# Two PSUM banks in one instruction: merged exponentials, normalisations and clamped sums in an attention and feed-forward kernel

## The chip, the cores and the metric

The kernel runs on one core of a Trainium2 chip. The metric is device time in microseconds, the median of several executions. The engines are TensorE (PE, with its weight loads shown as PEld), VectorE (DVE), ScalarE (ACT), GpSimd (POOL) and SyncE (SP); PSUM, into which TensorE writes, has eight banks of 512 float32 for each of 128 partitions.

## The reference

```python
# q, k, v: (4, 8, 768, 64); n_global 8, n_local 96
scores = scale * np.matmul(q, k.transpose(0, 1, 3, 2))
is_global = pos[None, :] < int(n_global)
is_local = (rel >= 0) & (rel < int(n_local))
keep = is_global | is_local
dist = np.where(is_global & ~is_local, float(n_local), np.abs(rel))
slopes = 2.0 ** (-8.0 * (np.arange(H) + 1) / H)
scores = scores - slopes[:, None, None] * dist[None, :, :]
scores = np.where(keep, scores, -1000000000.0)
scores = scores - np.max(scores, axis=-1, keepdims=True)
a = np.exp(scores)
a = a / (np.sum(a, axis=-1, keepdims=True) + 1e-09)
attn = np.matmul(a, v)                        # (4, 8, 768, 64)
x = attn.transpose(0, 2, 1, 3).reshape(3072, 512)
h = np.maximum(x @ w_in, 0.0)                 # w_in (512, 2048)
out = h * h @ w_out                           # w_out (2048, 512)
```

## The kernel before

The 3072 rows are worked in eight halves of 384 rows (three tiles of 128), two for each batch element. For each half the kernel loads q, k and v, turns q and k (the first batch on TensorE, later ones by transposing DMAs), forms the scores of each tile with its own block of keys and the block before (whose first 32 columns are replaced by the global keys), takes exponentials, multiplies them by a mask that holds the bias, multiplies by v, divides by the sum, and turns the result into `xt`. Layer 1 multiplies `xt` by w_in, clamps at zero and squares into `h2`; layer 2 multiplies by w_out. From the third half on, layer 1 is done by a scheme with seven block products in place of eight (`layer1_group`), and most of layer 2 too (`layer2_pair`); sums of inputs and of weights are formed on VectorE for them.

**Order.** The kernel lists its work twice. First, functions such as `score_unit`, `attend` or `layer1_group` list operations in a `Plan`: `plan.pe` for products on TensorE (numbered p0, p1, ...), `plan.add` and `plan.after` for work of the other engines (a number in one common list; its letter tells the engine: a ScalarE, d VectorE, s SyncE, g GpSimd) and `plan.load` for loads in GpSimd's queue (l0, l1, ...). `ORDER` is a table, and `by_table` emits the operations in its order; `l40^227` is a load that also waits for operation 227. Each engine works through its own entries in that order. The loads of the opening are numbered by `LOADING`, so that l1 to l3 are k and q of tiles 3 and 2, l7 and l8 q and k of tile 5, and l11, l13, l16 and l17 the four quarters of w_in.

**PSUM.** A product that begins an accumulation takes one or two banks. `idle_banks` (L225) sorts the banks whose readers are all done by the time at which they became idle, and takes the first ones. Each bank is a tile of its own, under the tag `ps0` to `ps7` (`bank`). Semaphores are placed by the framework, from which tiles an instruction reads and writes.

**The work around the change.**
- `score_unit` (L697) and, for the first batch, `score_tile` (L1390) write scores into two banks, one for each of two heads. Two `ACTIVATE` instructions (L721; L1426) take the exponentials, one for each bank.
- `attend` (L754) multiplies by v into one bank for each pair of heads. `norm` takes the reciprocal of the sums (L778) and multiplies (L781), once for each of the four pairs of heads. `to_x_by_dma` turns two of them at a time with one DMA (L796).
- `layer1_group` has the products p1, p5, p2, p6, p3, p7, p4. Bank "a" receives p1, then p6, p7 and p4; bank "c" a copy of p1's sum and p2; bank "f" p5 and p3. `keep` copies a partial sum to SBUF. p3 and p7 each end with a clamped sum on VectorE, `add_relu` (L990): the bank plus the kept partial sum, clamped at zero. p4 writes into bank "a" again, and needs p7's clamped sum to be done. Squares (L1012, L1014) follow when both parts of a block are there.

Of the kernel before, what the change touches and what calls it, by code (L numbers as in the profile page):

```python
# [9 lines left out]
FP32 = mybir.dt.float32  # L10
# [4 lines left out]
P = 128  # L15
# [33 lines left out]
ORDER = """d1 g2 a4 s8 p0 s10 a6 d12 a0 d13 l2 l1 a18 l3 d3 a30 d17 d15 d20 l4 a25 d14 a29 d9 a16 l0 d19 a26  # L49
d22 d21 d5 a23 p2 a28 l10 d11 p1 a24 p5 d7 l5 p3 l6 p10 d31 a32 a33 d34 l9 p6 a27 d35 p9 a39 p8 l8  # L50
d44 p11 d36 a40 p7 d43 l7 p4 a46 p13 d37 a41 p14 d45 l11 p12 d48 a42 p16 p17 d59 a47 l12 p15 a52 p25
d51 p19 l13 a49 d38 p28 p24 d55 a53 p20 l14 d69 p23 d64 a50 p34 d65 a60 l16 p31 d56 p21 a81 p22 d72
p27 l15 a61 p29 d58 p30 a57 p26 d70 a82 p33 l17 d68 p18 a71 a77 p35 d66 l23 p36 p32 d54 a86 d67 a85
p40 d62 p39 l18 d63 a97 d91 a73 p41 l19 d84 a78 d83 a74 p37 d79 l20 a98 d75 p44 l22 p38 d107 l21 d80
p47 d76 a89 p52 p48 d96 l27 a92 d111 p42 a93 l28 d106 a112 p43 l29 a119 p46 a113 d105 p45 a101 l30
d110 p53 d103 p55 p50 a120 p59 a90 d95 d116 a87 d100 p51 d99 d94 p57 d122 p54 d125 p65 p63 p49 d135
d121 p67 d146 a114 d128 a102 p61 p62 a104 d132 d117 a88 p75 d108 a129 p83 d115 a142 d109 p60 d209
a143 d118 d189 p64 a130 d273 d193 a138 p70 a136 p72 d159 p82 a133 d194 p71 d187 a134 p56 d160 a131
d190 a162 p69 d137 a186 p81 d161 l33 a123 d212 p74 d139 a165 d163 l25 a188 d156 p84 d205 a166 l31
d151 p73 a169 a184 d157 p85 l35 d206 a164 d167 a171 d147 p58 a168 l36 d196 p80 d124 l34 a126 p89  # L60
d148 p88 a181 p86 l32 d210 a202 d150 a182 p76 l24 d158 a170 d183 p77 a172 l26 d152 p87 a203 d174
a199 l37 p78 d154 a197 p79 p66 d204 a200 l38 a127 d207 p68 d185 a178 d149 a179 p90 a140 d180 p91
a213 d208 a175 d144 p94 a173 d201 a176 p92 d153 s220 d237 p100 a215 d195 a155 p102 s221 d211 d238
a214 p96 a224 d177 p95 a241 a141 p98 d225 p104 a216 s198 d226 p93 p97 a246 d223 a217 s227 a218 p103
d230 d222 p99 s231 a245 d240 p110 d239 p108 s219 l43 p111 a256 d244 a249 l44 p106 a257 d259 a250
d236 l40^227 p109 d247 p116 d228 p101 a252 l45 d251 a269 d258 p115 l41 a270 p114 d242 p113 a253 d192
l42 a262 d255 p117 a265 d232 p105 l46 d191 a272 a260 d233 p123 a266 l48^220 p118 a263 d280 p121 p122
d235 a274 l39 d234 p132 a278 d268 p128 a145 d279 p130 a287 d264 p126 a292 p127 d271 p125 a290 s327
p134 a285 d267 p139 d286 p135 d283 p133 a302 p136 s248 l47 d254 a295 p129 d296 s328 p143 a288 d293
p141 a284 p138 d297 p142 d304 p140 a289 p124 d300 s229 p137 a303 d294 p120 a306 d281 p146 a305 p144  # L70
d277 p147 a311 p131 a301 d307 p107 s282 d298 a329 p145 d291 p148 a309 p112 a308 d312 a399 d314 p151
p152 d313 p156 l51^282 s299 a330 p149 d310 p119 d315 a331 d322 a341 p150 s243 d316 a333 s261 l49^231
d275 a342 p168 d317 p165 a321 l52 a334 p153 d318 p155 a355 l53 a336 d332 p154 a337 d323 l50 d319
a359 p170 d324 l54 p160 d320 a361 p172 a350 p174 d338 a364 p161 p163 d366 a351 p164 a326 p176 d325
d340 p166 d436 p158 d369 a354 d335 a339 p169 a347 d356 p178 a367 p157 d360 p159 a371 d343 a344 p171
d348 a345 p181 d353 p180 s402 l56^327 a362 p182 a375 d374 p173 a372 p184 d346 p186 s403 a365 p162
d376 a357 p188 a382 d352 p192 d363 a380 p167 p179 a385 d391 s276 p175 s377 a373 p189 d358 a368 p190
a404 p185 d386 p193 s392 d388 d381 p183 p191 d393 a387 p187 l63 d389 p196 a383 p177 d390 a413 l59
p194 d378 a370 d384 a414 l74 p201 d379 a409 p202 p195 a423 l58 p199 d405 a426 d415 l62 p198 a427
d406 a424 d395 l55^377 p206 a410 d407 p200 a437 d416 l61^403 a421 d396 p211 a411 d408 p197 a420 l60  # L80
d397 p203 d481 p212 a417 d429 p204 a422 l75 d425 a445 a418 d484 p207 l66 d412 p205 a444 a438 d433
l57 a430 p213 d428 p216 d435 a446 d400 p220 l65 s434 a431 p214 p219 a455 d447 p215 a454 p227 d450
a448 s496 p222 d398 p225 d485 p218 a449 d486 p217 a461 d432 p210 a464 s497 a452 d419 a458 p224 d482
p231 a401 d460 p228 p229 d465 s349 l64 p221 a442 a453 p226 d466 p235 d456 p232 a462 p223 d469 a475
p239 d483 a451 d467 a571 p234 d459 a457 p208 p233 d473 a489 p237 a494 p209 d470 s474 a471 p230 d439
p241 a468 d440 a498 p242 s394 d478 s443 a500 s441 d463 p236 p238 d476 p249 a479 d472 p245 p244 a517
p240 d488 a501 d487 a505 p247 d499 a506 d477 l73^441 s495 a508 p246 d513 a518 d492 l71 d480 a509
p258 p248 d490 a533 l70 d511 p243 d519 p251 a514 l69 d491 a515 d520 p252 a502 p265 l72 p262 d542
a503 p260 p253 a538 l67 d536 p270 a525 p266 d507 a527 p267 l68 a543 d510 p257 a528 p268 d548 a532
p255 p271 d544 a530 p261 d493 a549 p273 d545 a546 p259 d537 p269 a552 p274 d534 p275 d516 p264 p276  # L90
a540 d547 p278 a556 p272 d554 a553 p254 a550 d535 s575 p250 a551 d559 d504 p282 s576 d521 p283 a565
p279 d523 a529 p281 a524 p277 d522 a563 p284 p286 d566 d560 p287 d568 a578 a567 d557 p280 p291 a564
d541 s558 d555 p263 d577 p285 p256 s526 d561 s512 p293 d583 a531 d569 p295 d595 a602 d539 p296 p292
a604 d570 a605 p298 d598 a596 a607 s597 p288 d599 s562 a608 p290 d606 p294 a585 d601 a586 p301 s574
d579 a592 d600 s573 a603 p297 a617 d609 p289 d614 p303 a588 d610 s584 d587 a593 s572 p306 a611 d580
d619 p307 a612 d623 p299 a589 d663 p310 p308 a615 d582 a624 d613 p300 d664 a625 p304 a629 p315 d590
a616 p312 d591 a621 p323 d581 d631 a635 p309 p302 a645 d627 p311 a618 p329 d630 p316 a628 p319 d594
p317 a636 p313 d640 p327 d637 a632 p305 a653 p321 d638 a650 p333 d622 a642 p322 p330 a644 d659 p320
p318 d654 p314 s660 a639 p325 d633 p326 a648 p332 d634 p335 s626 d658 s655 p324 d649 p331 d646 p334
p336 d656 a661 d641 a643 p328 p346 a667 d668 p351 a651 d682 p338 d657 a698 a692 d670 p353 d669 p355  # L100
d671 p357 d703 p337 a706 d665 a652 p361 d701 p350 a674 d711 p347 a672 p359 a673 d666 p363 p339 d708
d693 a697 p358 a647 p340 d707 a713 a662 p354 d677 p364 d675 p349 d683 a715 p342 s676 d702 d684 p352
p356 d699 a696 p362 p367 d687 a712 p365 d678 s688 p360 d704 a716 s620 p343 d714 a709 d710 p371 d679
p369 d685 p341 d705 d724 a719 p366 a689 d680 p368 a686 d717 p372 a700 p345 d720 d725 p370 d718 a691
p373 a721 p344 d737 d727 a726 d681 p348 d722 p374 d723 p383 d738 a728 p385 d756 a729 p377 a690 d733
p375 a741 d740 a759 d734 p378 d739 d694 d735 s695 p380 d730 d752 d736 p376 d742 d748 p379 d749 a731
d751 s732 d753 p381 p388 d754 p387 p386 a743 d744 a762 d755 a761 d745 p382 s746 p390 d747 p391 d760
p384 d765 d750 d764 p394 s766 a757 p389 a771 a772 s758 p392 d763 p393 d767 d769 s768 s770"""
# [28 lines left out]
class Plan:  # L137
# [7 lines left out]
    ENTER = 0.19  # L145
# [117 lines left out]
    def run(self):  # L263
        order = []
        self.in_rows = False
        for e, op in self.by_table() if ORDER else self.by_rank():
# [9 lines left out]
            if op.move is not None:  # L276
                there, long, back = op.move
                self.last_move = start
                self.landed = max(end + there, self.landed) + long
                op.done = self.landed + back  # L280
# [18 lines left out]
def kernel(  # L299
# [44 lines left out]
    def bank(shape, dtype, name, i=0):  # L344
        return ps_p.tile(shape, dtype, name=name, tag=f"ps{plan.now[i]}")
# [71 lines left out]
    def warm_up(e):  # L417
        ps = bank([P, 512], FP32, "warm")
        for _ in range(8):
            nc.tensor.matmul(ps, lhsT=zero[:, 0:P], rhs=zero, start=True, stop=True)  # L420
# [217 lines left out]
    def turn(x, a):  # L638
        state = {}

        def emit(e):
            state["ps"] = trp = bank([P, 2, HT, P], FP16, "trp")
# [54 lines left out]
    def score_unit(x, unit):  # L697
        bt, sp = x.bt, []
# [217 lines left out]
    def layer1_group(x, g):  # L916
# [69 lines left out]
        def give(job, name, which, n, kept=None):  # L986
# [20 lines left out]
            if len(done) < 2:  # L1007
                return ready
# [676 lines left out]
```

## Time and profile before

| | |
|---|---|
| median of 3 runs | 200.1 us (200.0 to 201.06) |
| profiled execution | 200.26 us, span 198.5 us |
| TensorE | 190.9 us busy (96%), 2428 matmuls, granted clock 0.999 |
| VectorE | 178.7 us (90%), 445 instructions |
| ScalarE | 153.6 us (77%), 332 instructions |
| GpSimd | 66.6 us (34%), 82 instructions |
| DMA | 27.53 MB, mean 139 GB/s |

The profile is of one execution. The span runs from the first to the last instruction; 1.76 us of that execution's time lie outside of it. A line of the groups names the kernel's line, the engine, the operation, what it writes and reads, how often, its busy time, the mean duration in ns, and the idle time of the engine ahead of it with what ended it. Busy time of TensorE counts overlapping matmuls once.

### The profile page before, as it was taken

To read this page: it belongs to the slowest core of one execution; us is meant where nothing else is said; L and a number is where in the kernel's file an instruction comes from. 1 tells how busy PE (TensorE), PEld (TensorE's weight loads), DVE (VectorE), ACT (ScalarE), POOL (GpSimd) and SP (SyncE) were. 2 spreads that over 40 slices of the span, in tenths; PEclk is the share of its full clock that TensorE was granted. 3 is DMA by queue.
4 is the path that set the end of the run, shared out by engine and by line. 5 is a ranking of instruction groups with operands and counts; after the bars stand their busy time and mean duration, and the time that the engine had idled before them with its cause. 6 is when DMAs were issued, how large, how long until landed. Compare 5 with 4: busy or idle time off the path is not lost.

```text
span 198.5 us, 6069 instructions
## 1 busy us (share of the span) xinstructions
PE 190.9 (96%) x2428; PEld 166.7 (84%) x2428; DVE 178.7 (90%) x445; ACT 153.6 (77%) x332; POOL 66.6 (34%) x82
## 2 busy tenths in 40 slices
PE   7997999999999999999999999999999999999992
PEld 2775988866987897799989997999889998999992
DVE  7898898999998999998999997999999998898842
ACT  6798766989897989999999987976599758366210
POOL 8996544098006900920696000910000000000000
PEclk9999999999999999999999999999999999999999
DMA  5999999999999999998999996999542050120223
GB/s 160 178 148 191 196 183 170 207 196 155 137 211 125 126 135 271 175 142 138 180 149 150 134 195 166 84 105 156 153 129 81 3 132 5 53 106 3 106 82 132
DMA packets 106604, 27.53 MB, mean 139 GB/s; under 512 B 96720, under 2 KB 103632, under 8 KB 106576
## 3 DMA queue, kind: packets, MB, share of 16 engines
q0 software_dynamic: 74944, 13.11, 86.0%
q1 hardware_dynamic: 30432, 13.45, 33.9%
q10 hardware_dynamic: 1200, 0.59, 1.1%
q8 instruction: 19, 0.31, 0.7%
q14 instruction: 9, 0.07, 0.1%
HBM read 27.26 MB, written 6.29 MB: 169 GB/s over the span
## 4 chain that ended last, share of the span: by engine, by line
PE 83%; DMA 5%; POOL 4%; DVE 4%; ACT 1%; issue 1%; POOLq 0%; DVEq 0%
PE yps L1143 32%; PE hps L929 28%; PE hps L818 9%; PE sp L708 4%; PE av L769 4%; DMA w_mix<-in_k_dram 4%; PE yps L1059 4%; POOL w_mix L488 2%; DMA xt<-tm 2%; POOL v L488 1%; DVE tm L1471 1%; DVE vb L354 1%; PE trp L646 1%; DVE hr L990 1%; POOL sk L488 1%
## 5 line engine op out<-in xcount | busy, mean ns | idle before, releaser
L1143 PEld LDWEIGHTS <-h 128*128 128x128 f16 x376 | 33.9, 98 | 4.1
L721 ACT ACTIVATE ex<-sp 128x512 f16<-128x512 f32 x66 | 35.6, 615 | 1.5 <-PE sp L708 1.3
L929 PEld LDWEIGHTS <-w_in_sb 128*128 128x128 f16 x384 | 32.4, 98 | 2.1 <-issue 0.5
L1143 PEld LDWEIGHTS <-mixed 128*128 128x128 f16 x272 | 25.3, 98 | 3.0
L488 POOL DMA_DIRECT2D v<-in_v_dram x24 | 21.5, 921 | 16.5 <-DMA xt<-tm 16.2
L990 DVE CUSTOM_DVE_ANT_0 hr<-hps,kept 128x384 f16<-128x384 f32 x48 | 25.2, 553 | 1.4 <-ACT y L352 0.5
L929 PEld LDWEIGHTS <-in_mix 128*128 128x128 f16 x288 | 24.3, 98 | 0.6 <-DVE x_mix L908 0.3
L488 POOL DMA_DIRECT2D sq<-in_q_dram x19 | 17.0, 900 | 21.9 <-DMA q<-sq 20.3
L488 POOL DMA_DIRECT2D sk<-in_k_dram x19 | 17.1, 907 | 20.9 <-DMA xt<-tm 11.7
L818 PE MATMUL hps<-xt,w_in_sb 128*128 128x256 f16 (+2 forms) x224 | 23.4, 258 | 0.0
L929 PE MATMUL hps<-xt,w_in_sb 128*128 128x192 f16 x192 | 22.8, 246 | 0.2 <-DMA xt<-tm 0.2
L996 ACT ACTIVATE hr<-hps 128x384 f16<-128x384 f32 x35 | 17.0, 496 | 7.6 <-PE hps L929 7.1
L352 ACT COPY y<-yps 128x256 f32<-128x256 f32 (+2 forms) x36 | 12.9, 369 | 12.7 <-PE yps L1143 12.5
L352 ACT COPY kept<-hps 128x384 f32<-128x384 f32 x41 | 19.0, 491 | 4.6 <-PE hps L929 3.9
L1143 PE MATMUL yps<-w_mix,h 128*128 128x256 f16 (+1 forms) x192 | 22.6, 264 | 0.0
L929 PE MATMUL hps<-x_mix,w_in_sb 128*128 128x192 f16 x192 | 22.1, 246 | 0.3 <-DVE hr L990 0.3
L1143 PE MATMUL yps<-w_out_sb,h 128*128 128x256 f16 (+1 forms) x184 | 22.4, 268 | 0.0
L1143 PE MATMUL yps<-w_mix,mixed 128*128 128x256 f16 (+1 forms) x184 | 22.2, 268 | 0.0
L929 PE MATMUL hps<-x_mix,in_mix 128*128 128x192 f16 x192 | 21.9, 246 | 0.0
L745 DVE TENSOR_TENSOR phat<-ex,mask 128x1024 f16<-128x1024 f16 (+1 forms) x36 | 20.9, 597 | 0.3 <-ACT ex L721 0.3
L818 PEld LDWEIGHTS <-w_in_sb 128*128 128x128 f16 x224 | 17.7, 98 | 3.6 <-DMA w_in_sb<-in_moe_w_in_dram 0.2
L1012 ACT ACTIVATE h<-hr 128x768 f16<-128x768 f16 x23 | 19.3, 846 | 0.1
(112 smaller groups left out, 378.5 us busy)
## 6 DMA issues: line engine op xcount, KB each, us to landing
out_dram<-y SPq DMA_DIRECT2D x23, 256.0 KB, 2.5
v<-in_v_dram POOLq DMA_DIRECT2D x24, 128.0 KB, 6.4
sk<-in_k_dram POOLq DMA_DIRECT2D x19, 128.0 KB, 5.4
sq<-in_q_dram POOLq DMA_DIRECT2D x19, 128.0 KB, 5.9
w_in_sb<-in_moe_w_in_dram POOLq DMA_DIRECT2D x4, 512.0 KB, 11.2
w_out_sb<-in_moe_w_out_dram POOLq DMA_DIRECT2D x4, 512.0 KB, 10.7
y<-in_k_dram ACTq DMA_DIRECT2D x2, 256.0 KB, 4.9
y<-in_q_dram SPq DMA_DIRECT2D x2, 256.0 KB, 4.3
```

What stands on the lines that cost most here:

```text
L352: nc.scalar.copy(out=out, in_=in_)
L488: dma = nc.gpsimd.dma_start(out=dst, in_=src[x.b, :, r0 + t * P:r0 + (t + 1) * P, :] .rearrange("h p d -> p h d"))
L708: nc.tensor.matmul(sp[h][:, i, :], lhsT=lhsT, rhs=x.q[rows, r % HT, a, :], start=i == 0, stop=True, skip_group_check=True)
L721: nc.scalar.activation(out=st["ex"][:, h], in_=sp[h], func=AF.Exp, scale=scale)
L745: eng(e).tensor_tensor(out=x.phat[a][:, :, t0:t0 + n], op=ALU.mult, in0=st["ex"][:, :, i0:i0 + 2 * n].rearrange("p e (t b) c -> p e t (b c ...
L769: nc.tensor.matmul(av[:, h, j, :], lhsT=lhsT, rhs=rhs, start=h == 0 and (j, before) == blocks[0], stop=before or r == 0, skip_group_check= ...
L818: nc.tensor.matmul(st["ps"][:, i * n:(i + 1) * n], lhsT=w_in_sb[:, kk, m * P:(m + 1) * P], rhs=x.xt[:, kk, c0:c1], start=i == kk == 0, sto ...
L929: nc.tensor.matmul(st[name][:, i * HC:(i + 1) * HC], lhsT=left(i, kk), rhs=right(kk), start=fresh > 0 and i == kk == 0, stop=kk == KK - 1, ...
L990: nc.vector._custom_dve(TENSOR_ADD_SAT, out=hidden(which)[:, :, cols], in0=sums(name), in1=st[kept], s0=LARGEST, s1=0.0)
L996: nc.scalar.activation(out=o, in_=i, func=AF.Relu)
L1012: nc.scalar.activation(out=h2, in_=hr, func=AF.Square)
L1143: nc.tensor.matmul(st[bank_name][:, 0:n], lhsT=a(m), rhs=b(m)[:, cols], start=fresh > 0 and m == 0, stop=m == HK - 1, skip_group_check=not ...
```

## The change

All of PSUM becomes one tile of eight banks, and `bank` gives out a view of one of them. `two_banks` gives a view of two banks, whichever they are. With it, one instruction reads both banks: one exponential for the two heads of a score unit, one reciprocal and one product for two pairs of heads, and one clamped sum for p3 and p7 together (`give_two`, which waits for both products and both kept sums). The normalisation is listed at the second `attend` of its pair; its DMA waits for that one operation. The kept sums and the hidden values (`hr`) of a group lie in one tile each, and the exponentials of the first batch are masked in place. `ORDER` is replaced as a whole (1164 entries where there were 1244); the planner adds 0.6 us (`LATER`) to its expected landing times once they pass 15 us, and its costs for the merged operations are 0.87 to 1.13 us. `LOADING`, `OPENING`, `PLACES` and `idle_banks` stay.

```diff
-    def bank(shape, dtype, name, i=0):
-        return ps_p.tile(shape, dtype, name=name, tag=f"ps{plan.now[i]}")
+    banks = ps_p.tile([P, 8, 512], FP32, name="ps", tag="ps")
+
+    def bank(shape, dtype, i=0):
+        flat = banks[:, plan.now[i]]
...
+    def two_banks(i, j, n):
+        return banks[:, i::j - i][:, 0:2, 0:n]
...
-        for h in range(2):
-            def exp(e, h=h):
...
-                nc.scalar.activation(out=st["ex"][:, h], in_=sp[h], func=AF.Exp, scale=scale)
-            exps.append(plan.add({"ACT": 0.505}, exp, [job] + exps))
+        def exp(e):
+            st["ex"] = phat_p.tile([P, 2, 4, P], FP16, name="ex", tag="ex", bufs=4)
...
+                                 in_=two_banks(*held, 4 * P), func=AF.Exp, scale=scale)
+        exps = [plan.after(job, {"ACT": 0.87}, exp)]
...
-        x.norms[a] = plan.after(job, {"DVE": 0.74}, norm)
+        x.norms[pair] = plan.after(jobs[0], {"DVE": 1.13}, norm, jobs[1:])
+        jobs[1].users[0].append(x.norms[pair])
...
+        def give_two(one, two):
+            def add_relu(e):
+                ps = two_banks(st["held", "f"], st["held", "a"], 2 * HC)
+                nc.vector._custom_dve(
+                    TENSOR_ADD_SAT, out=hidden()[:, :, :, HC:2 * HC],
+                    in0=ps.rearrange("p b (m c) -> p b m c", c=HC),
+                    in1=st["kept"].rearrange("p b (m c) -> p b m c", c=HC), s0=LARGEST, s1=0.0)
+            op = plan.after(two, {"DVE": 0.96}, add_relu, [one, ops["kept", 0], ops["kept", 1]])
...
         def p3():
-            job = run("f", 0, mixed_weight(3), plain(1, 1), [ops["keep5"], in_mix_ops[g][3]])
-            give(job, "f", 0, 1, "keep2")
+            ops["p3"] = run("f", 0, mixed_weight(3), plain(1, 1),
+                            [ops["kept", 1], in_mix_ops[g][3]])

         def p7():
-            job = run_mixed("a", 0, mixed_weight(2), 2, [ops["keep2"], in_mix_ops[g][2]])
-            ops["c22"] = give(job, "a", 1, 1, "keep5")
+            job = run_mixed("a", 0, mixed_weight(2), 2, [ops["kept", 0], in_mix_ops[g][2]])
+            ops["c22"] = give_two(ops["p3"], job)
```

The first loads, in the order of the old and of the new table (k2 is tile 2 of k, c1 the second quarter of w_in; tiles 0 and 1 of q and k come by other queues):

```
before: k2 k3 q2 v0 v1 k4 q3 q4 v2 k5 q5 c1 v3 c0 v4 c3 v5 c2
after:  q2 k2 v0 q3 k3 v1 k4 q4 v2 c2 q5 k5 v3 c1 v4 c0 v5 ... c3
```

More of the change, by code (lines that the diff above doesn't have):

```diff
@@ L278, in run @@
                 self.last_move = start
[L279 removed]
+                before, self.landed = self.landed, max(end + there, self.landed) + long
+                self.landed += self.LATER if before <= 15.0 < self.landed else 0.0
                 op.done = self.landed + back
@@ L417, in warm_up @@
     def warm_up(e):
-        ps = bank([P, 512], FP32, "warm")
+        ps = bank([P, 512], FP32)
         for _ in range(8):
@@ L697, in score_unit @@
     def score_unit(x, unit):
-        bt, sp = x.bt, []
+        bt, sp, held = x.bt, [], []
         def emit(e):
-            sp.extend(bank([P, 4, P], FP32, "sp", h) for h in range(2))
+            held.extend(plan.now)
+            sp.extend(bank([P, 4, P], FP32, h) for h in range(2))
             warm(sp[0].rearrange("p i c -> p (i c)"))
@@ L759, in emit @@
         def emit(e):
-            st["av"] = av = bank([P, 2, HT, D + 1], FP32, "av")
-            warm(av.rearrange("p e t d -> p (e t d)"))
+            av = bank([P, HT, 2, D + 1], FP32)
+            x.held[a] = plan.now[0]
+            warm(av.rearrange("p t e d -> p (t e d)"))
             for h in range(2):
@@ L787, in attend, with norm @@
             x.buf0.used_by(job)
-        x.norms[a] = plan.after(job, {"DVE": 0.74}, norm)
+        x.av_jobs[a] = job
+        pair = a // 2
+        if 2 * pair + 1 - a % 2 not in x.av_jobs:
+            return
+        jobs = [x.av_jobs[2 * pair + i] for i in range(2)]
+        def norm(e):
+            held = [x.held[2 * pair + i] for i in range(2)]
+            av = two_banks(*held, 2 * HT * (D + 1)).rearrange("p a (n d) -> p a n d", d=D + 1)
+            rec = tm_p.tile([P, 2, 2 * HT], FP32, name="rec", tag="rec")
+            nc.vector.reciprocal(out=rec, in_=av[:, :, :, D])
+            x.tm[pair] = tm_p.tile([P, 2, HT, 2, D], FP16, name="tm", tag="tm", bufs=3)
+            nc.vector.tensor_tensor(
+                out=x.tm[pair].rearrange("p a t e d -> p a (t e) d"), in0=av[:, :, :, 0:D],
+                in1=rec[:, :, :, None].to_broadcast([P, 2, 2 * HT, D]), op=ALU.mult)
+        x.norms[pair] = plan.after(jobs[0], {"DVE": 1.13}, norm, jobs[1:])
+        jobs[1].users[0].append(x.norms[pair])
     def to_x_by_dma(x, pair):
-        norms = [x.norms[2 * pair + i] for i in range(2)]
+        norms = [x.norms[pair]]
         def emit(e):
@@ L813, in emit @@
             if k0 == 0:
-                st["ps"] = bank([P, 512], FP32, "hps")
+                st["ps"] = bank([P, 512], FP32)
                 warm(st["ps"])
@@ L925, in emit @@
                 for i in range(fresh):
-                    st[(name, "c")[i]] = bank([P, 512], FP32, "hps", i)
+                    st["held", (name, "c")[i]] = plan.now[i]
+                    st[(name, "c")[i]] = bank([P, 512], FP32, i)
                 for i in range(2):
@@ L998, in relu, with given @@
                     eng(e).tensor_scalar(out=o, in0=i, scalar1=0.0, scalar2=None, op0=ALU.max)
-            done = st.setdefault(("done", which), [])
-            if kept:
-                done.append(plan.after(job, {"DVE": 0.55}, add_relu, [ops[kept]]))
-                bufs[kept].used_by(done[-1])
-            else:
-                done.append(plan.after(job, {"ACT": 0.41, "DVE": 0.48}, relu))
-            hr_bufs[which].used_by(done[-1])
-            ready = done[-1]
-            if len(done) < 2:
-                return ready
+            given(which, plan.after(job, {"ACT": 0.41, "DVE": 0.48}, relu))
+        def give_two(one, two):
[6 more added lines that the diff above has]
+            op = plan.after(two, {"DVE": 0.96}, add_relu, [one, ops["kept", 0], ops["kept", 1]])
+            one.users[0].append(op)
+            kept_buf.used_by(op)
+            for which in range(2):
+                given(which, op)
+            return op
+        def given(which, op):
+            done[which].append(op)
+            if op not in hr_buf.users:
+                hr_buf.used_by(op)
+            if len(done[which]) < 2:
+                return
             def square(e):
-                hr, h2 = hidden(which), x.h2[:, m0 + which * far:m0 + which * far + 2]
+                hr = st["hr"][:, which].rearrange("p (m c) -> p m c", c=HALF)
+                h2 = x.h2[:, m0 + which * far:m0 + which * far + 2]
                 if e == "ACT":
@@ L1056, in emit @@
             if m0 == 0:
-                st["ps"] = bank([P, 512], FP32, "yps")
+                st["ps"] = bank([P, 512], FP32)
             for m in range(m0, m0 + 4):
@@ L1380, in emit @@
         def emit(e):
-            st["sp", before] = pair = [bank([P, NPAIR, P], FP32, "sp", i) for i in range(2)]
+            st["held", before] = list(plan.now)
+            st["sp", before] = pair = [bank([P, NPAIR, P], FP32, i) for i in range(2)]
             warm(pair[0].rearrange("p a c -> p (a c)"))
@@ L1397, in emit @@
             if not added:
-                st["sp", before] = [bank([P, NPAIR, P], FP32, "sp", i) for i in range(2)]
+                st["held", before] = list(plan.now)
+                st["sp", before] = [bank([P, NPAIR, P], FP32, i) for i in range(2)]
                 warm(st["sp", before][0].rearrange("p a c -> p (a c)"))
@@ L1417, in score_tile, with ex @@
                 u.append(job)
[L1418 to L1430 removed]
+        buf = Buffer("ex", 4)
+        st["bufs"] = [*st.get("bufs", []), buf]
+        def ex(e):
+            st["ph", before] = phat_p.tile([P, 2, NPAIR, P], FP16, name="ex", tag="ex", bufs=4)
+            nc.scalar.activation(out=st["ph", before].rearrange("p h a c -> p h (a c)"),
+                                 in_=two_banks(*st["held", before], NPAIR * P), func=AF.Exp,
+                                 scale=scale)
+        exps = [plan.after(job, {"ACT": 0.88}, ex)]
+        buf.used_by(*exps)
         def weigh(e, a0):
```

231 lines of the change are left out of this document (101 added, 130 removed).

## The prediction

> **What bounds the kernel now.** I read the page's busy times first, then the windows by stage, then TensorE's waits, then the chain of waits, and last the costs by line and form.
>
> ```profile
> span 198.5 us, 6069 instructions
> PE 190.9 (96%) x2428; PEld 166.7 (84%) x2428; DVE 178.7 (90%) x445; ACT 153.6 (77%) x332; POOL 66.6 (34%) x82
> 0.00:20.00 20.00, 16.85 (x240) 11.93 (x241) 17.25 (x56) 15.62 (x34) 17.17 (x25) 1.00 1.84 170
> 20.00:27.00 7.00, 6.81 (x104) 6.23 (x104) 6.38 (x21) 5.62 (x14) 3.57 (x5) 1.00 1.53 193
> 27.00:100.00 73.00, 73.00 (x924) 61.47 (x926) 69.20 (x166) 65.13 (x139) 32.13 (x38) 1.00 1.61 169
> 100.00:150.00 50.00, 49.76 (x648) 45.14 (x643) 47.73 (x112) 42.49 (x95) 13.70 (x16) 1.00 1.32 140
> 150.00:194.50 44.50, 44.16 (x522) 41.74 (x520) 37.45 (x93) 24.71 (x56) 0.00 (x0) 1.00 0.22 69
> 194.50:198.50 4.00, 0.36 (x7) 0.18 (x4) 0.67 (x2) 0.00 (x0) 0.00 (x0) 0.93 0.24 84
> PE warm L420 <- DVE early L1542: 1.2, 1, 1.2
> PE trp L1363 <- DMA w_mix<-in_k_dram: 0.9, 1, 0.9
> PE hps L929 <- DVE hr L990: 0.3, 1, 0.3
> ```
>
> The first column behind each stretch is its length, the next TensorE's busy time. From 27 to 194.5 us (167.5 us) TensorE is busy for 73.00 + 49.76 + 44.16 = 166.92: it stands still for 0.58 us in all. All it loses is at the ends: 3.15 us before 20, 0.19 up to 27, 3.64 behind 194.5. In the middle its longest wait for a reader of PSUM (L990) is 0.3 us. So VectorE (90%) and ScalarE (77%) are hidden behind TensorE; work taken off them is worth nothing there, and a wait added in front of a matmul is paid in full.
>
> **What the merging saves.** The forms:
>
> ```profile
> L721 ACT ACTIVATE ex<-sp 128x512 f16<-128x512 f32 x66 | 35.6, 615 | 1.5 <-PE sp L708 1.3
> L352 ACT COPY kept<-hps 128x384 f32<-128x384 f32 x41 | 19.0, 491 | 4.6 <-PE hps L929 3.9 <-DVE hr L990 0.6
> L990 DVE CUSTOM_DVE_ANT_0 hr<-hps,kept 128x384 f16<-128x384 f32 x48 | 25.2, 553 | 1.4 <-ACT y L352 0.5 <-PE hps L929 0.4 <-ACT ex L721 0.2
> L1206 DVE TENSOR_TENSOR y<-yps,y 128x256 f32<-128x256 f32 x22 | 9.0, 421 | 4.9 <-PE yps L1143 4.6 <-ACT ex L721 0.2
> L781 DVE TENSOR_TENSOR tm<-av,rec 128x384 f16<-128x384 f32 x24 | 13.4, 558 | 0.8
> L778 DVE RECIPROCAL rec<-av 128x6 f32<-128x6 f32 x24 | 4.5, 188 | 0.0
> ```
>
> ScalarE: 128 more columns cost 615 - 491 = 124 ns, so 1024 columns are 615 + 4 x 124 = 1.11 us for two times 0.615. Over 33 pairs that is 4.0 us, over the 11 of the first batch 1.3. But two exponentials in a row already overlap: where four run together the timeline gives 2.08 us, 0.52 each, so the saving lies between 0 and 5.3 us; I take the lower half, as the pairs do run back to back.
> VectorE: 128 more columns cost 553 - 421 = 132 ns, so a clamped sum of 768 is 0.95 us; 48 x 0.553 - 24 x 0.95 = 3.7 us saved. A normalisation pair is 2 x (0.558 + 0.188) = 1.49 now and about 0.95 + 0.20 = 1.15 then: 12 x 0.34 = 4.1 us saved.
> Counting the letters in the two tables, ScalarE has 326 entries before and 267 after, 59 fewer, of which merging explains 44; VectorE has 21 fewer where merging takes 36. So 15 evacuations and squares go from ScalarE to VectorE, 15 x about 0.5 = 7.5 us, and VectorE stays at 90%. On the path all of this is zero, by the 0.58 us above. The cover is TensorE's own work; without it the price of a late VectorE is what is late.
>
> **Steps that move.** p3's clamped sum now waits for p7, and p4 for the 0.95 us sum in place of 0.55. Adding up the products that the new table puts between the later of p3 and p7 and their p4 (0.33 us for an L929 product, 0.87 for an L1143, 0.30 to 0.37 for an attend, from their starts in the trace), the least of the 24 gaps is 1.33 us. That covers 0.95 with 0.38 left, where before p4 could stand straight behind p3. The first normalisation of a pair waits for the second attend; both feed one transposing DMA (L796), which waited for the later one already. `kept` and `hr` hold as much as before (two groups; six halves against five).
>
> The loads in POOL's queue are put in another order. Before, w_in's first quarter follows tile 5's q and k; now one quarter goes ahead of them, and q2 ahead of k2. The first layer 1 product, which waited for w_in at 20.0 us, may start earlier, while the last k tile, which TensorE waits for at 17.05 (0.9 us), comes one quarter later: at least the 0.8 us of an issue, at most the 3.0 us that 512 KB take at the 170 GB/s of this stretch (q5, k5 and the v tiles are queued behind it). Between 10 and 20 us TensorE is idle for 1.6 us. Gain: at most these 1.6 and the 0.58 of the middle; at the other end a loss of 3.0. I take 1.6 of gain, as layer 1 work can fill in.
>
> **What it adds.** All PSUM tiles become one tile. The framework that places the semaphores compares two accesses to one tile by the stretch from the first bank touched to the last. Written out for a few matmuls on one tile of eight banks: a read of banks 1 and 6 in one instruction makes a later matmul into bank 2 wait for it, and itself waits for an earlier one there, but leaves bank 0 alone; a read of banks 1 and 2 leaves bank 4 alone. A VectorE read of a bank in between waits for ScalarE too. So each merged instruction holds up every matmul into the banks between its two. The change doesn't touch the rule by which the planner hands out banks (`idle_banks`: longest idle first), which knows no neighbours.
>
> The price, laid on the trace of before: I took the banks that the planner hands out there, merged each pair at its own start, and looked for the first product that starts inside the merged instruction's time and writes to a bank strictly in between. An example:
>
> ```profile
> 144.12 2.08 ACT L721 ACTIVATE ex<-sp 128x512 f16<-128x512 f32 x4
> 144.69 1.92 PE L1143 MATMUL yps<-w_mix,mixed 128*128 128x256 f16 x16
> ```
>
> Of the four exponentials, the last two start at 144.60 and read banks 6 and 0; the product at 144.69 writes bank 4. Merged, they end at about 145.67, and the product stands 0.98 us.
> From 27 us on, such a product exists for 15 of 33 exponentials (8.3 us in sum), 8 of 24 clamped sums (5.2) and 4 of 12 normalisations (3.4), at 1.07 us (between 2 x 0.52 and 1.11), 0.95 and 1.20 us (1.15 and the hand-over). Overlapping stalls counted once, 16.3 us. If a merged instruction also starts later where a product in between is still running, 22.9. Before 27 us it is 3.4 to 5.2 us more, most of it beside waits for loads; I take 0 there. 16.3 is the value I take for the middle, since the new order has other coincidences, not fewer: it packs the same 395 products as tightly. From below I bound it by half, 8 us, for an order that happens to avoid them.
>
> [...]
>
> **Sum.** The profiled execution took 200.26 us, 1.76 more than its span, 0.16 above the median of 200.1. 200.26 + 16.3 - 1.6 = 215.0. Bounds: 200.26 + 8 - 2.2 = 206.1, and 200.26 + 22.9 + 5.2 + 3.0 = 231.4 if all goes wrong at once, which I cut to 226, as late loads and stalls before 27 us would largely stand in the same time. A difference of 0.5% (1 us) is about what a measurement of this kernel can tell.
>
> **Rivals.**
> 1. The table avoids the stalls (24%, faster). If whoever ordered it let each instruction wait by the program's own semaphores, products into banks in between stand elsewhere, and what is left is the gain at the opening: 200.26 - 1.6 = 198.7, at best 198.1. For it: the p4 gaps fit the longer sum (1.33 us at least), so the order was made for these durations, and 17 loads carry a gate where 8 did. It decides once less than 2.6 us of the stalls is left (1.6 + 1.0), four of the 27. Against it: `Plan.ready` and `idle_banks` model one wait per bank, and the diff adds nothing to either.
> 2. Nothing moves (5%): stalls few, and what the opening wins the longer sums lose; 200.3.
> 3. A worse form of the forecast, within its 71%: VectorE at 90% held by ScalarE's reads of banks in between. Nine of 24 sums have such a read beside them, about 0.5 us each. That is 4.5 us more, about 219.5.
>
> **How the numbers follow.** The forecast has 71%; its own range is 206 to 226. The range as a whole goes down to 198, most of the first rival, so that no more than 2 in 10 is left out. Faster 0.24, same 0.05, slower 0.71.
>
> **What would show it.** If right: in the waits, TensorE waits for ScalarE's exponentials and VectorE's sums and normalisations some 25 times, 0.3 to 1 us each, 12 us or more together, against 0.3 now; its busy share falls to about 90% with the same 2428 matmuls; ScalarE's exponential is near 1.1 us x44, the clamped sum 0.95 us x24. The opening is right if layer 1 starts before 20 us and less is lost before 27. It is wrong if TensorE's waits between 27 us and the end stay under 3 us; then the first rival holds, and the time is read from the opening.

## Result: 242.7 us, a fifth slower

The changed kernel takes 242.69 us (median of 4 runs, 242.26 to 245.04), the kernel before 200.25 us beside it: a ratio of 1.2135, 95% interval 1.2049 to 1.222. The direction was forecast, the size was not: 215.0 was predicted, and 242.7 lies above the range of 198 to 226. The profiled execution took 242.89 us, with a span of 241.1.

The page's first lines and the windows of the changed kernel (length of the stretch, then the busy time of TensorE, its weight loads, VectorE, ScalarE and GpSimd, the granted clock, the DMA share and GB/s):

```profile
span 241.1 us, 5991 instructions
PE 197.1 (82%) x2426; PEld 166.9 (69%) x2426; DVE 181.0 (75%) x414; ACT 148.8 (62%) x271; POOL 66.7 (28%) x82
0.00:20.00 20.00, 14.86 (x206) 9.76 (x206) 13.63 (x47) 13.95 (x25) 17.15 (x26) 1.00 1.67 172
20.00:27.00 7.00, 5.44 (x90) 4.56 (x91) 5.41 (x20) 5.77 (x10) 4.02 (x6) 1.00 1.68 188
27.00:60.00 33.00, 30.02 (x340) 23.40 (x338) 27.33 (x70) 25.41 (x47) 13.06 (x16) 1.00 1.62 157
60.00:100.00 40.00, 31.05 (x405) 25.27 (x403) 30.19 (x66) 24.80 (x43) 14.94 (x17) 1.00 1.47 118
100.00:150.00 50.00, 38.92 (x492) 34.07 (x490) 34.75 (x70) 32.81 (x61) 14.91 (x17) 1.00 1.08 121
150.00:200.00 50.00, 42.16 (x536) 37.97 (x534) 40.25 (x80) 30.02 (x55) 2.63 (x3) 1.00 0.41 74
```

The span grew by 42.6 us. TensorE does the same products (2426 records against 2428) but stands still for 241.1 - 197.1 = 44.0 us where it stood for 7.6, which is 36.4 us of the 42.6; the other 6.2 are in its busy time. No engine has become the bound: VectorE fell from 90% to 75%, ScalarE from 77% to 62%. From 60 to 150 us TensorE stands for 20 us of the 90, and no other engine is busier than it (VectorE 64.9 us, ScalarE 57.6). That is the picture of engines that wait for each other in turn.

TensorE's waits in the changed kernel (us in total, times, longest):

```profile
PE ps L946 <- DVE hr L1016: 6.0, 7, 1.2
PE ps L946 <- ACT ex L729: 4.5, 5, 1.1
PE ps L946 <- DVE tm L800: 3.7, 4, 1.4
PE ps L717 <- ACT ex L729: 3.7, 5, 1.1
PE ps L1166 <- DVE hr L1016: 3.6, 4, 1.4
PE ps L946 <- ACT ps L360: 2.4, 2, 1.6
PE ps L1166 <- ACT ex L729: 1.7, 2, 1.5
```

L729 is the merged exponential, L1016 the merged clamped sum, L800 the merged normalisation. L946 is a layer 1 product: nothing in the computation lets it wait for an exponential or a normalisation, and L1166, of layer 2, uses no result of either of its releasers directly. Only the banks connect them. The timeline shows both directions of it. First an exponential that waits for a product, and the next product that waits for the exponential:

```profile
48.22 1.03 PE L1082 MATMUL ps<-w_out_sb,h 128*128 128x512 f16 x4
49.29 1.02 ACT L729 ACTIVATE ex<-ps 128x1024 f16<-128x1024 f32 x1 [1.05 <-PE ps L1082]
50.36 0.34 PE L717 MATMUL ps<-q,k 64*128 64x128 f16 x6 [1.11 <-ACT ex L729]
```

The exponential reads the scores in banks 2 and 7. It starts 1.05 us late, when a layer 2 product (L1082) into bank 5 has ended. The next product, scores of another unit for bank 4, then stands for the whole exponential. Then a longer chain, where the wait passes over three engines:

```profile
108.50 1.04 PE L1166 MATMUL ps<-w_out_sb,h 128*128 128x256 f16 x8
109.68 0.96 DVE L1016 CUSTOM_DVE_ANT_0 hr<-ps,kept 128x768 f16<-128x768 f32 x1 [1.95 <-PE ps L1166]
110.67 0.74 ACT L360 COPY ps<-ps 128x384 f32<-128x384 f32 x2 [2.03 <-DVE hr L1016]
111.19 0.33 PE L946 MATMUL ps<-xt,w_in_sb 128*128 128x192 f16 x2 [1.65 <-ACT ps L360]
```

VectorE idles for 1.95 us before the clamped sum of banks 0 and 6, held by a layer 2 product into bank 5; ScalarE idles for 2.03 us before its copy from bank 2 to bank 3, held by the sum; TensorE stands 1.65 us for the copy, which fills the bank that this product adds to and is late for no reason of its own.

I sorted every stop of TensorE over 0.15 us in this trace by the banks that the program's instructions name. From 27 us on it is held by a merged read of two other banks, with its own in between, **27 times, 24.0 us** in sum (exponentials 9.2, clamped sums 9.8, normalisations 3.9, exponentials of the first batch 1.1); each time it starts 0.05 to 0.06 us after that read has ended. Another 12 stops, 9.1 us, are for a late reader of its own bank or a late copy into it, as in the chain above; before the change there was one such stop, of 0.3 us. Before 27 us a merged read holds it 3 times, 3.6 us. The merged instructions are themselves held by products in banks in between: 10 times on ScalarE (8.5 us) and 14 times on VectorE (14.5 us). In 4 more cases (4.1 us) it is an instruction of the other of these two engines, on a bank in between, that holds them.

The forms, to set beside those of before:

```profile
L729 ACT ACTIVATE ex<-ps 128x1024 f16<-128x1024 f32 x33 | 32.9, 1026 | 14.5 <-PE ps L1166 3.8 <-PE ps L717 3.4 <-PE ps L1082 2.5
L1016 DVE CUSTOM_DVE_ANT_0 hr<-ps,kept 128x768 f16<-128x768 f32 x24 | 22.7, 954 | 10.5 <-PE ps L946 3.7 <-PE ps L778 3.2 <-PE ps L1166 2.3
L800 DVE TENSOR_TENSOR tm<-ps,rec 128x768 f16<-128x768 f32 x12 | 11.5, 958 | 0.4
L798 DVE RECIPROCAL rec<-ps 128x12 f32<-128x12 f32 x12 | 2.7, 228 | 9.1 <-PE ps L1166 4.4 <-PE ps L946 2.3 <-ACT ex L729 1.8
```

What follows the last bar is idle time of the engine ahead of the group: 14.5 us before exponentials (1.5 before the change), 10.5 before clamped sums (1.4), 9.1 before reciprocals (0.0).

### The profile page after: what moved, and what is told of

The parts are those of the page before. It is cut to its first block, busy times and chain, and to the rows that moved or that the text cites. A ratio compares the mean times of both kernels' runs of the same rounds, so it can differ in the third digit from the quotient of the medians.

```text
span 241.1 us, 5991 instructions
## 1 busy us (share of the span) xinstructions
PE 197.1 (82%) x2426; PEld 166.9 (69%) x2426; DVE 181.0 (75%) x414; ACT 148.8 (62%) x271; POOL 66.7 (28%) x82
## 5 line engine op out<-in xcount | busy, mean ns | idle before, releaser
L946 PEld LDWEIGHTS <-w_in_sb 128*128 128x128 f16 x384 | 32.9, 98 | 16.6 <-issue 14.0
L729 ACT ACTIVATE ex<-ps 128x1024 f16<-128x1024 f32 x33 | 32.9, 1026 | 14.5 <-PE ps L1166 3.8
L1166 PEld LDWEIGHTS <-h 128*128 128x128 f16 x376 | 34.3, 98 | 9.3 <-issue 5.7
L946 PE MATMUL ps<-xt,w_in_sb 128*128 128x192 f16 x192 | 23.2, 245 | 9.9 <-ACT ex L729 2.5
L496 POOL DMA_DIRECT2D sq<-in_q_dram x19 | 17.1, 904 | 48.7 <-DMA q<-sq 28.0
L1016 DVE CUSTOM_DVE_ANT_0 hr<-ps,kept 128x768 f16<-128x768 f32 x24 | 22.7, 954 | 10.5 <-PE ps L946 3.7
L1166 PEld LDWEIGHTS <-mixed 128*128 128x128 f16 x272 | 25.2, 98 | 7.1 <-issue 3.7
L946 PEld LDWEIGHTS <-in_mix 128*128 128x128 f16 x288 | 24.4, 98 | 6.7 <-issue 5.0
L496 POOL DMA_DIRECT2D sk<-in_k_dram x19 | 16.9, 895 | 39.4 <-DMA xt<-tm 37.3
L1008 ACT ACTIVATE hr<-ps 128x384 f16<-128x384 f32 x38 | 18.4, 493 | 11.7 <-PE ps L946 8.8
L946 PE MATMUL ps<-x_mix,in_mix 128*128 128x192 f16 x192 | 22.5, 246 | 3.5 <-DVE hr L1016 2.6
L946 PE MATMUL ps<-x_mix,w_in_sb 128*128 128x192 f16 x192 | 22.9, 246 | 3.1 <-DVE tm L800 1.4
L1166 PE MATMUL ps<-w_out_sb,h 128*128 128x256 f16 (+1 forms) x184 | 23.0, 268 | 2.6 <-DVE hr L1016 2.2
L1166 PE MATMUL ps<-w_mix,mixed 128*128 128x256 f16 (+1 forms) x184 | 22.4, 268 | 2.4 <-ACT ex L729 1.5
L1166 PE MATMUL ps<-w_mix,h 128*128 128x256 f16 (+1 forms) x192 | 22.5, 263 | 2.0 <-DVE y L1229 1.6
L834 PE MATMUL ps<-xt,w_in_sb 128*128 128x128 f16 (+2 forms) x224 | 23.5, 257 | 0.4 <-DVE xt L362 0.4
L753 DVE TENSOR_TENSOR phat<-ex,mask 128x1024 f16<-128x1024 f16 (+1 forms) x36 | 20.8, 594 | 3.7 <-ACT ex L729 3.7
## 6 DMA issues: line engine op xcount, KB each, us to landing
w_out_sb<-in_moe_w_out_dram POOLq DMA_DIRECT2D x4, 512.0 KB, 11.5
```

The lines of the kernel that those rows point to most:

```text
L496: dma = nc.gpsimd.dma_start(out=dst, in_=src[x.b, :, r0 + t * P:r0 + (t + 1) * P, :] .rearrange("h p d -> p h d"))
L729: nc.scalar.activation(out=st["ex"].rearrange("p h i c -> p h (i c)"), in_=two_banks(*held, 4 * P), func=AF.Exp, scale=scale)
L753: eng(e).tensor_tensor(out=x.phat[a][:, :, t0:t0 + n], op=ALU.mult, in0=st["ex"][:, :, i0:i0 + 2 * n].rearrange("p e (t b) c -> p e t (b c ...
L834: nc.tensor.matmul(st["ps"][:, i * n:(i + 1) * n], lhsT=w_in_sb[:, kk, m * P:(m + 1) * P], rhs=x.xt[:, kk, c0:c1], start=i == kk == 0, sto ...
L946: nc.tensor.matmul(st[name][:, i * HC:(i + 1) * HC], lhsT=left(i, kk), rhs=right(kk), start=fresh > 0 and i == kk == 0, stop=kk == KK - 1, ...
L1008: nc.scalar.activation(out=o, in_=i, func=AF.Relu)
```

## The experiments

The theory after this reading: what costs is an instruction that reads two banks with others in between; the new order, the one tile and the merging itself cost little. The rivals: the new order is to blame; one tile makes everything wait for everything; the instructions are simply longer and come later.

All experiments on the changed kernel replace `two_banks` by one function, and loop over what it yields; with an empty `MERGE` each bank is read by an instruction of its own, and all else stays. A time without a ratio beside it is one single execution.

```diff
-    def two_banks(i, j, n):
-        return banks[:, i::j - i][:, 0:2, 0:n]
+    def parts(kind, i, j, n):
+        i, j = PERM[i], PERM[j]
+        if kind in MERGE and (not NEAR or abs(i - j) == 1):
+            return [(slice(0, 2), banks[:, i::j - i][:, 0:2, 0:n])]
+        return [(slice(h, h + 1), banks[:, b:b + 1, 0:n]) for h, b in enumerate((i, j))]
```

### 1. The new order, nothing merged

```diff
+MERGE = ()
```

> The changed kernel with its new order, its one PSUM tile and its merged operations, but each merged operation issues two instructions, one for each bank. Theory W (a merged read makes the products into the banks between its two wait): TensorE's waits for readers fall from 35 us to under 3 us, and the time to 198 to 202 us. Rival O (the new order and the steps it moves, the later clamped sums and the loads, cost the time): the stalls stay, over 225 us. Rival L (a merged instruction is longer and so gives its two banks back later): as W here, 198 to 205; told apart by permuting the banks.

Measured: 203.13 us, a ratio of 1.015 to the kernel before (1.0093 to 1.0207). So 39.6 of the 42.4 us come from merging, 3 from the rest. The theory's range ended 1 us below; that the order as such is to blame, at over 225, is out. Its page and windows:

```profile
span 201.0 us, 6107 instructions
PE 192.0 (96%) x2426; PEld 165.9 (83%) x2426; DVE 181.3 (90%) x462; ACT 148.4 (74%) x315; POOL 67.1 (33%) x82
0.00:20.00 20.00, 16.89 (x238) 11.59 (x239) 15.49 (x53) 16.20 (x35) 17.21 (x25) 1.00 1.68 173
20.00:27.00 7.00, 6.57 (x108) 5.60 (x106) 6.11 (x23) 6.94 (x15) 4.33 (x6) 1.00 1.68 188
27.00:100.00 73.00, 72.06 (x902) 59.79 (x901) 69.67 (x170) 60.46 (x129) 31.60 (x38) 1.00 1.66 169
```

TensorE is back at 96%. VectorE's busy time is 181.3 us with 48 more instructions, against 181.0 merged, and ScalarE's 148.4 against 148.8: merging saved neither engine anything in sum. The durations added up do fall, from 213.2 to 205.4 us on VectorE and from 175.8 to 165.0 on ScalarE, but neighbouring instructions overlap by about as much less.

### 2. The old order, merged and not

The old table, with each merged exponential at the place of the first of its two and each merged sum or normalisation at the place of the later; entries that must wait for one are moved back, by up to 14 places. Once with all merged, once with `MERGE = ()`.

> The changed code with the merged instructions, in the order of the old table (its entries carried over one by one; a merged one stands where the first exponential or the later sum or normalisation stood; entries that must wait are moved back by up to 14 places). Theory W: coincidences between merged reads and products in between are as many as in the new order, 225 to 245 us. Rival O: 199 to 205 us, as the old order has no fault. Rival L: 205 to 240, unspecific.

> As the run before, with two instructions for each merged operation. Theory W and L: within 2 us of the kernel before, 199 to 203, since only the place of the clamped sums and one PSUM tile are left of the change. Rival O: 199 to 203 as well; above 205 the single tile or the later sums would have a price of their own.

Measured: 252.16 and 217.04 us. Both are above what was expected. The trace of the second shows one large reason. Even split, the clamped sums still wait for p3 and p7 together, and in the old table p4 stands straight behind:

```profile
PE ps L959 <- DVE hr L1029: 8.6, 8, 2.2
```

So the split kernel in the old order is 16.9 us slower than the kernel before (217.04 - 200.14). These stops are 8.6 us of it, all for the product's own bank; TensorE's busy time is 4.9 us longer (195.8 against 190.9), and the rest I have not traced. The new order, which keeps products between the later of p3 and p7 and their p4, takes 14 us less than the old one with the same operations (217.04 - 203.13). Merging adds 35.1 us to the old order and 39.6 to the new, so its price depends little on which of these two orders it is.

### 3. One kind merged at a time

```diff
+MERGE = ('exp', 'tile')      # the exponentials; ('add',) the clamped sums; ('norm',) the normalisations
```

> New order, only the exponentials merged (44 instructions), sums and normalisations one instruction for each bank. Theory W: of the 27.0 us in which TensorE is held by merged reads in the changed kernel, exponentials have 14.0; with the knock-on that makes 27.0 us of stalls into 42.6 us of time (x1.58), 22 us over the split kernel, 216 to 226 us. Rival O: no change from the changed kernel. Rival L: exponentials hold banks 0.5 us longer, at most a few us, 200 to 210.

> New order, only the clamped sums merged (24 instructions). Theory W: 9.0 of the 27.0 us in which TensorE is held by merged reads, times 1.58, is 14.3 us over the split kernel's 203.1: 213 to 222 us. Rival L: under 207, since the sum that p4 waits for ends at the same time merged or split (0.95 against 2 x 0.55).

> The changed kernel with only the normalisations merged; exponentials and clamped sums read one bank at a time. Theory (the costs of the three kinds are separate waits and nearly add): the three together cost 242.7 - 203.1 = 39.6 us, exponentials alone 20.8 and clamped sums alone 14.0, so normalisations are left with 4.8; and 3.9 us of TensorE's stops in the changed kernel, which grow there by 39.6 / 25 in time. Together 203.1 + 4.8 to 6.2 = 208 to 209.5 us (range 206 to 212). Rival (the kinds hold each other up, so that most of the last 4.8 us comes only from their being together): under 205 us.

Measured: 223.88, 217.16 and 209.02 us, which is 20.8, 14.0 and 5.9 us over the kernel with nothing merged; the sum, 40.7, is close to the 39.6 of all three together. Each kind costs by itself, in the range that waits on banks in between gave, and the costs add. So do TensorE's stops for a merged read with its bank in between: 14.4, 8.7 and 4.6 us, together the 27.6 us of the changed kernel (24.0 and the 3.6 before 27 us). That the sums and the normalisations would cost little alone (under 207, under 205) is out.

### 4. The same order and instructions, other bank numbers

Each bank number that the planner gives is replaced through a table; which operations share a bank, their order and their lengths stay as they are. Only what lies in between changes.

```diff
+PERM = [4, 1, 3, 5, 7, 2, 0, 6]      # few products in between
+PERM = [4, 1, 7, 0, 3, 2, 6, 5]      # many
```

> The changed kernel with its bank numbers permuted (planner's bank 0 is bank 4 of the tile, and so on: 4, 1, 3, 5, 7, 2, 0, 6), nothing else. Same instructions, lengths, order and times of release. Laid on the trace of the split kernel, merged reads hold up products in between for 18.4 us (29 of 80) instead of 32.4 (40 of 80) with the numbers as they are. The changed kernel lost 39.6 us to the split one, 1.22 times 32.4. Theory W: 203.1 + 1.22 x 18.4 = 225, 219 to 232 us. Rival L (merged instructions give banks back later): no change, 241 to 244.

> The changed kernel with the permutation 4, 1, 7, 0, 3, 2, 6, 5 of its bank numbers, which by the same count puts 52.4 us of products (60 of 80 merged reads) in between. Theory W: 203.1 + 1.22 x 52.4 = 267, 255 to 280 us. Rival L: 241 to 244.

Measured: 229.0 and 268.49 us, both inside what was expected. With the numbers of the changed kernel it is 242.7, so a renaming of banks moves the time by 39.5 us. This is the sharpest of the tests: an explanation by longer or later instructions gives the same time for all three (241 to 244). Sorted as above, over the whole run, a merged read with TensorE's bank in between holds it 18 times (14.6 us) at 229.0 us, 30 times (27.6) at 242.7 and 47 times (48.7) at 268.5; with nothing merged it never does. The renaming without merged reads was not run. TensorE's waits of the slow one:

```profile
PE ps L957 <- ACT ex L737: 9.6, 9, 2.1
PE ps L957 <- DVE hr L1027: 7.5, 9, 1.2
PE ps L724 <- ACT ex L737: 6.9, 5, 2.0
PE ps L1178 <- ACT ex L737: 4.7, 5, 1.1
```

These are the kinds of waits of the changed kernel, only more: layer 1 (L957) waits for exponentials 9 times where it did 5. Not all of the 268.49 is waits, though: TensorE's clock fell in this run (below), and the 11.3 us that its busy time grew over the changed kernel (208.4 - 197.1) belong largely to that: compared matmul by matmul, 10.6 us of them lie where the granted clock was lower (0.63 to 0.51 by windows from 10 to 18 us, 0.50 from 22 to 34).

### 5. Merged where the two banks are neighbours

The planner prefers, among the banks that are idle by then, two that lie side by side; a pair that still has banks in between is read in two instructions. 46 of the 80 pairs are merged.

```diff
+NEAR = True
...
+        elif op.takes == 2 and not op.wide:
+            near = [(max(good[i], good[i + 1]), i) for i in range(7) if i in good and i + 1 in good]
```

> New order; the planner prefers neighbouring banks for what is read together, where they are idle in time, and an operation is one instruction where its two banks are neighbours (46 of 80) and two where not. No merged read has a bank in between. Theory W: no stall for merged reads, 198 to 204 us; whether it beats 200.1 depends on what the new order's opening gains, and on the shorter VectorE work. Rival L: the 46 longer instructions cost something, 205 to 225.

Measured: 202.94 us, a ratio of 1.013 (1.0097 to 1.0163). The forms:

```profile
L762 ACT ACTIVATE ex<-ps 128x1024 f16<-128x1024 f32 x24 | 24.2, 1032 | 3.4 <-PE ps L749 3.3
L1053 DVE CUSTOM_DVE_ANT_0 hr<-ps,kept 128x768 f16<-128x768 f32 x11 | 10.5, 955 | 0.4
```

24 exponentials and 11 clamped sums read two banks at once, as long as in the changed kernel (1.03 and 0.955 us), and the idle time before them is gone (3.4 for their own scores, 0.4). A merged read with nothing in between costs nothing here. It brings nothing either: the time is that of the kernel with none merged (202.94 against 203.13 us).

### 6. What the remaining 3 us are not

The kernel before with one change, its banks as views of one tile; and the kernel of experiment 5 where a split clamped sum reads the bank that p4 writes next ahead of the other.

```diff
+    banks = ps_p.tile([P, 8, 512], FP32, name="ps", tag="ps")
     def bank(shape, dtype, name, i=0):
-        return ps_p.tile(shape, dtype, name=name, tag=f"ps{plan.now[i]}")
+        flat = banks[:, plan.now[i]]
```

```diff
-                for c, ps in parts("add", st["held", "f"], st["held", "a"], 2 * HC):
+                for c, ps in parts("add", st["held", "f"], st["held", "a"], 2 * HC)[::-1]:
```

> The kernel before, with its own order, its loads and all its instructions of one bank each; only the banks are now views of one tile of eight. Theory (what costs is an instruction that reads two banks with others in between; one tile alone costs nothing): 200.1 us, within 199.5 to 200.8, TensorE 96% busy. Rival (one tile makes accesses to different banks wait for each other even where each touches one bank, which would explain the 3 us by which the new order with split reads stays behind the kernel before): 202 to 204 us.

> As the kernel whose planner prefers neighbouring banks (202.94 us), but where a clamped sum is split it reads bank a, which p4 writes next, ahead of bank f. Theory (the 3 us by which the new order without banks in between stays behind the kernel before come partly from p4, which now waits behind two sums in a row): 0.5 to 1.5 us less, 201.4 to 202.4 us. Rival (p4 is covered by the products ahead of it, 1.33 us at least, and the rest comes from other small waits): 202.6 to 203.3 us.

Measured: 199.67 us (ratio 0.9982, 0.9968 to 0.9997) and 202.73 us (1.0135, 1.0101 to 1.017). One tile costs nothing here, where every instruction touches one bank; the 0.2% by which it is faster is below what I would build on. And the bank that p4 waits for is not the reason, as far as the 13 of the 24 sums that are split there tell: 202.73 is the 202.94 of experiment 5. Where the 3 us of the new order go stays open. By the profile of experiment 1 TensorE idles 1.4 us longer than before and is busy 1.1 us longer, in many small stops, none over 0.6 us behind the opening.

No version of the new order beats the kernel before: TensorE, busy for 96%, is its bound, and merging takes work only from engines that TensorE hides.

## Why the prediction was right in sign and wrong in size

**The mechanism was right.** The prediction said that a read of two banks makes products in between wait and waits for them, and put this down to the way in which the framework places the program's semaphores. The renamed banks show the first (229.0 to 268.5 with the same work). For the second, the neighbours (202.94) show that two banks in one read cost nothing by themselves, the one tile (199.67) that the shared tile costs nothing by itself, and TensorE's 27 stops end each time with the read of the other banks, 0.05 to 0.06 us behind it. With one bank in each read, beside products into others, TensorE is busy for 96% (192.0 of 201.0 us in experiment 1).

**The steps that failed are the price of the stalls, 16.3 us, and the terms that were put at nothing beside it.** The forecast was short by 27.9 us (242.89 - 215.0). The price of the stalls is 7.7 of them. Its count came out: 27 stops were predicted from the order of before, and 27 are there in the new one. That the two are equal is partly luck, since 15, 8 and 4 for exponentials, sums and normalisations became 11, 11 and 5. But each stop is 0.89 us long (24.0 / 27) where the prediction had 0.60 (16.3 / 27). It let every merged read start at its own time and charged only what was left of it when the product came. In the chip's run the read has often been held first by something in a bank in between, 28 times on both engines together, and so it ends later; at 49.29 it is 1.05 us late. Of the reads behind the 27 stops 14 had been held so, and their stops are 1.05 us long on average, as long as a whole read; the stops for the other 13 are 0.72. The prediction had this as its second figure, 22.9, and took the smaller. 22.9 is close to the 24.0, though that too was counted on the order of before.

**What was left at zero came on top**, and it is the larger part, 20.2 us of the 27.9. The sum against the profiled 242.89:

| term | predicted | measured |
|---|---|---|
| products in between, from 27 us on | 16.3 | 24.0 |
| late readers of a product's own bank, or late copies into it | 0 | 8.8 more than before |
| idle time before 27 us | -1.6 with the opening's gain | 3.4 more than before |
| TensorE's busy time | 0 | 6.2 more |
| rest, by difference | 0 | 0.2 |
| sum | 14.7 | 42.6 |

The second row is the third rival in a wider form: instructions of one of the two engines that wait for a merged read of the other, on banks in between. That happens 12 times on ScalarE and 7 times on VectorE, and some of their products then wait. The rival priced it at 4.5 us, for VectorE alone. The third row is two steps. Stalls before 27 us were taken to hide beside the waits for loads; three of them cost 3.6 us. And the gain of the opening did not come. In the order with nothing merged the first layer 1 product does start earlier, at 18.29 us, where it starts at 20.03 before the change and at 20.47 in the changed kernel; so "layer 1 starts before 20 us" was right for the order and wrong for the kernel. But no less time is lost: before 27 us TensorE stands for 3.5 us with nothing merged, against 3.3 before the change. The fourth row is a cost that I had not thought of. In a stream the matmuls overlap: in the changed kernel 192 of a kind that lasts 0.245 us on average (L946, `xt` by w_in) are busy for 23.2 us together. Behind a stop there is none before to overlap with: at 111.19 the first two, of that kind, take 0.33 together, so the second adds only some 0.08. With nothing merged the busy time is 1.1 us over that of before, so some 5.1 us belong to the 42 stops, an estimate of 0.12 us each; no run tests this row by itself.

**Its range** took in most of the worse cases singly but cut their sum: 231.4 "if all goes wrong at once" was cut to 226 with the reason that stalls and late loads would stand in the same time. They added instead, as the three kinds do in experiment 3, and even 231.4 lies below the result, since the late readers and the busy time are not in it.

**The other steps.**
- *Durations.* The clamped sum was put at 0.95 us and takes 0.954, the normalisation at 0.95 + 0.20 and takes 0.958 + 0.228; the exponential at 1.11 and takes 1.026.
- *Savings.* The groups' busy time, merged against split: 34.7 + 11.5 to 32.9 + 11.1 for the exponentials (2.2 us; lower half of 5.3 predicted), 24.1 to 22.7 for the clamped sums (1.4; 3.7 predicted), 13.4 + 4.4 to 11.5 + 2.7 for the normalisations (3.6; 4.1 predicted). On the path they are worth nothing, as predicted: experiment 5 has most of them and no gain. VectorE stays at 90% in the new order, as predicted, while nothing holds it.
- *p4.* The least gap of 1.33 us covers the joint sum: with nothing merged TensorE's waits, listed down to 0.2 us, have no layer 1 product of a group that waits for a clamped sum. Experiment 2 shows what the cover is worth where it is missing: 8.6 us of stops for these sums, in a kernel that is 16.9 us slower; the prediction said that it mattered but gave it no number.
- *First rival* (the table avoids the stalls, 198.7): no. 27 stops were forecast, and 27 are there. Even where they are avoided, in experiment 5, the result is 202.9, since the new order is 3 us slower by itself.

## What to carry to other kernels

Before one instruction reads two buffers that it didn't read together, ask what the framework takes for the region that it touches: here it is the stretch from the first bank to the last, and everything in between becomes a false dependency in both directions. If pairs are merged, let the allocator give out neighbours, and merge only where it could. In pricing such waits, take the version in which the held instruction is itself held first, and add the readers behind it: in the changed kernel's chain at 108.50 us the false wait was handed on from engine to engine, 1.95 us on VectorE, 2.03 on ScalarE and 1.65 on TensorE.

## What the runs showed of the hardware beyond that

TensorE's granted clock did not stay full in every run. In the slow renaming of experiment 4 the granted clock (third column from the right) was 0.942 over the run, 0.999 in the changed kernel; by windows:

```profile
7.00:20.00 13.00, 8.27 (x105) 6.67 (x104) 6.15 (x18) 6.25 (x9) 12.04 (x15) 0.74 2.07 169
20.00:33.00 13.00, 9.61 (x109) 7.26 (x109) 5.56 (x19) 6.20 (x9) 7.15 (x9) 0.55 1.83 181
33.00:60.00 27.00, 25.63 (x315) 20.84 (x313) 22.89 (x65) 20.15 (x40) 6.30 (x8) 0.96 0.82 101
```

From 20 to 33 us 109 matmul records keep TensorE busy for 9.61 us at a clock of 0.55; between 22 and 34 us it is 0.50. From 6 to 10 us it is 1.00, with TensorE busy for 2.99 of the 4.00 us, and from 10 to 14 us 0.63, with 1.80 busy: eight score products (L1444) take 0.40 us at 9.25, and 0.61 at 11.09, behind a stop of 1.11 us. The longest of the listed waits in this run is 2.1 us. What lowers the clock the runs do not show: the changed kernel, busy for 2.42 us from 10 to 14 us and with a stop of 1.58 us that ends at 13.67, kept 1.00 in this stretch, and so did the old order with all merged (experiment 2), busy for 2.35 to 2.48 us in each 4.00 from 10 to 26 us. The other renaming of experiment 4, the one of 229.0 us, was below full for a while too (0.57 between 14 and 18 us).
